# Weight and slab loads in paced pieces of 128 to 256 KB in place of transfers of 512 KB to 1 MB

## The chip, the cores and the metric

One core of one Trainium2 chip. The time is that of the device for one execution, in microseconds (us), the median of several runs; lower is better. One execution of each kernel was also profiled, and the trace of that execution is what the views below read.

## The reference

A transformer layer in bf16, batch 1, 2048 tokens of width 1024: attention with 32 query heads of 32 and one shared key and value head, then a gated feed-forward of width 3584.

```python
h  = x + A(layernorm(x))          # A: q = x@wq, k = x@wk, v = x@wv, softmax(q k^T / sqrt(32)) v, then @ wo
h2 = h + B(layernorm(h))          # B: (sigmoid(x@w_gate) * (x@w_up)) @ w_down
```

## The kernel before

The kernel holds a list scheduler in Python. It builds the instruction list of each engine ahead of time, from assumed durations, and then emits the five lists with semaphore waits. TensorE interleaves scores (`S_ps`), P·V blocks and the feed-forward, so that ScalarE's exponentials (`Pr<-S_ps`) never lack work. The feed-forward goes in 8 chunks of 256 tokens, and each chunk reads all of `w_gate` and `w_up` again: 14 slabs of 1 MB per chunk (a gate half and an up half of 512 KB), through a ring of five slabs. A slab is requested when the one five before it has been used:

```python
def load_wd(f, n, deps):                       # 7 times, 1 MB each
    wd_ld.append(dma(lambda: SP.dma_start(
        wd_sb[:, f:f + n, :], B_w_down[f * P:(f + n) * P, :].rearrange("(a p) n -> p a n", p=P)),
        f"wd{f}", n * P * D * 2, deps, prio=4))

def load_slab(s, deps):                        # 112 times, two transfers of 512 KB
    ...
    for w, W in ((0, B_w_gate), (1, B_w_up)):
        ops.append(dma(lambda w=w, W=W: SP.dma_start(
            wgu[:, sl, w, :, :], W[:, pi * SW:(pi + 1) * SW].rearrange("(a p) f -> p a f", p=P)),
            f"sl{sl}{w}", D * SW * 2, deps, prio=4))

def after(b, last):                            # after a gate (w == 0) or up (w == 1) group
    if w == 0:
        ...                                    # tanh on ScalarE
        return [tanh_of[s]]
    e = ...                                    # (tanh + 1) * up on VectorE
    load_slab(s + NSLAB, [last])               # both halves together
```

All these transfers are issued by SyncE, in the order of its list. Nothing in the kernel asks for instructions: the trace shows 189 fetches of 16 KB, spread over the run, in a DMA queue of their own (q8, 3.10 MB). They keep step with TensorE: in 200 to 250 us it starts 2,370 matmuls and weight loads and there are 9 fetches, in 1100 to 1150 us 785 and 3; over the run it is one fetch per 255 (48,282 by 189).

The softmax here doesn't subtract the row's maximum and nothing guards it: scores larger than these inputs give would overflow.

## Time and profile before

| | before |
|---|---|
| time, median of the first 3 runs (lowest to highest) | 1196.02 us (1194.79 to 1198.01) |
| profiled execution: span, granted TensorE clock | 1192.8 us, 0.997 |
| exponentials (1024), mean | 1035 ns |
| slab matmuls (3584), mean | 274 ns |
| slab loads, issue to landing, median | gate 4.1, up 5.5 us |

The prediction below shows the lines of the profile that matter. One habit helps in reading them: the share of busy time says which engine is the bound (TensorE, 95%), and the waits of that engine, the small ones too, say what there is to gain. Waits of other engines need not cost anything: here VectorE waits 213.6 us for TensorE's blocks (`Oc<-F_ps`) while TensorE is busy for 95%.

### The profile page before, as it was taken

What the parts mean: (1) busy time and instruction counts of PE and PEld (TensorE: products, weight loads), DVE (VectorE), ACT (ScalarE), POOL (GpSimd) and SP (SyncE); (2) the same over time, 40 slices, a digit from 0 to 9 for tenths busy, and PEclk for the clock granted to TensorE, in tenths of its full rate; (3) what the DMA queues carried; (4) which work ended last, traced back from release to release, by engine and by line L of the source; (5) the groups of instructions that cost most, each with busy time, mean ns of one, the idle gap of its engine ahead of it and who ended that gap; (6) DMA issues with size and microseconds to landing.
All of it is one profiled execution on the core that took longest, in us unless ns stands there. A gap on an engine that the chain in (4) does not pass through costs nothing.

```text
span 1192.8 us, 52074 instructions
## 1 busy us (share of the span) xinstructions
PE 1138.6 (95%) x24020; PEld 775.2 (65%) x24141; DVE 843.1 (71%) x1539; ACT 1041.8 (87%) x1188; POOL 50.4 (4%) x84
## 2 busy tenths in 40 slices
PE   8899899999999999999998899999999999999998
PEld 5745577776576756775576655776576746775784
DVE  8677767787887678777776678777868787776221
ACT  6799899999998999999998999999999999995110
POOL 4100000000000000000000000000000000000000
PEclk9999999999999999999999999999999999999999
DMA  8765501665155632655054652656155723654470
GB/s 247 188 198 154 170 21 47 181 173 130 43 160 140 179 82 71 178 165 147 25 151 136 162 117 58 186 146 172 29 152 149 186 58 98 182 159 111 126 210 18
DMA packets 286025, 158.15 MB, mean 133 GB/s; under 512 B 34672, under 2 KB 276336, under 8 KB 285808
## 3 DMA queue, kind: packets, MB, share of 16 engines
q1 hardware_dynamic: 283728, 154.69, 47.7%
q8 instruction: 189, 3.10, 1.1%
q10 hardware_dynamic: 2080, 0.13, 0.1%
q14 instruction: 28, 0.23, 0.1%
HBM read 140.64 MB, written 7.34 MB: 124 GB/s over the span
## 4 chain that ended last, share of the span: by engine, by line
PE 83%; ACT 6%; DVE 5%; issue 4%; DMA 1%; POOL 1%; SPq 0%; DVEq 0%
PE F_ps L348 70%; PE S_ps L348 13%; ACT Pr L547 5%; DVE Ts L565 1%; DMA hnT<-hn 1%; DVE st L289 1%; DVE st L291 1%; POOL dsb L308 0%; DMA ring<-in_A_x_dram 0%; DVE Oc L610 0%; DVE Oc L608 0%; DVE ring L328 0%; POOL zb L303 0%; ACT ring L332 0%; POOL rstd L310 0%
## 5 line engine op out<-in xcount | busy, mean ns | idle before, releaser
L547 ACT ACTIVATE Pr<-S_ps 128x1024 bf16<-128x1024 f32 x1024 | 969.2, 1035 | 45.4 <-PE S_ps L348 44.5
L348 PE MATMUL F_ps<-hnT,ring 128*128 128x256 bf16 x3584 | 441.8, 274 | 9.3 <-issue 4.4
L348 PEld LDWEIGHTS F_ps<-hnT,ring 128*128 128x128 bf16 x3584 | 330.7, 98 | 76.4 <-issue 12.3
L565 DVE TENSOR_TENSOR Ts<-Pr 128x1024 bf16<-128x1024 bf16 x512 | 342.1, 683 | 14.8 <-ACT Pr L547 10.7
L348 PE MATMUL S_ps<-QTb,kT 32*128 32x128 bf16 x8192 | 209.9, 217 | 20.8 <-issue 16.7
L348 PEld LDWEIGHTS S_ps<-QTb,kT 32*128 32x128 bf16 x8192 | 119.7, 93 | 149.1 <-ACT Pr L547 67.4
L348 PE MATMUL F_ps<-zone,hact 128*128 128x512 bf16 x822 | 199.5, 380 | 6.2 <-issue 5.3
L608 DVE COPY Oc<-F_ps 128x256 f32<-128x256 f32 x128 | 54.3, 424 | 213.7 <-PE F_ps L348 213.6
L565 DVE TENSOR_TENSOR Ts<-Ts 128x1024 bf16<-128x1024 bf16 x256 | 170.5, 667 | 1.5
L348 PE MATMUL F_ps<-Pr,Vb 128*32 128x128 bf16 x8192 | 138.7, 220 | 2.1 <-issue 1.3
L348 PEld LDWEIGHTS F_ps<-zone,hact 128*128 128x128 bf16 x896 | 78.9, 98 | 90.8 <-issue 1.2
L348 PEld LDWEIGHTS F_ps<-Pr,Vb 128*32 128x32 bf16 x8192 | 115.8, 97 | 25.1 <-issue 8.1
L737 ACT ACTIVATE tnh<-F_ps 128x512 f32<-128x512 f32 x112 | 67.6, 603 | 65.0 <-PE F_ps L348 64.8
L610 DVE RECIPROCAL Oc<-Oc 128x128 f32<-128x128 f32 x128 | 121.1, 946 | 0.2
L741 DVE SCALAR_TENSOR_TENSOR hact<-tnh,F_ps 128x512 bf16<-128x512 f32 x112 | 76.0, 678 | 54.7 <-PE F_ps L348 53.5
L348 PE MATMUL F_ps<-zone 128*128 128x256 bf16 (+2 forms) x497 | 71.1, 287 | 5.9 <-ACT QTb L235 2.2
L348 PE MATMUL F_ps<-wo_sb,OT 128*128 128x512 bf16 x227 | 58.7, 381 | 3.1 <-issue 2.5
L348 PEld LDWEIGHTS F_ps<-zone 128*128 128x128 bf16 x512 | 38.0, 97 | 28.4 <-ACT QTb L235 3.0
L303 POOL TENSOR_SCALAR zb<-mvb 128x1 bf16<-128x1 bf16 (+1 forms) x25 | 10.3, 414 | 1057.1 <-DVE mvb L299 1057.1
L348 PE MATMUL F_ps<-Ts,ones 128*32 128x128 bf16 x2048 | 51.5, 219 | 1.9 <-issue 1.9
L348 PE MATMUL F_ps<-kT,ident 128*128 128x256 bf16 x337 | 43.9, 279 | 0.0
L773 DVE SCALAR_TENSOR_TENSOR h_sb<-F_ps,h_sb 128x512 bf16<-128x512 f32 x32 | 21.6, 676 | 30.6 <-PE F_ps L348 30.2
(44 smaller groups left out, 341.3 us busy)
## 6 DMA issues: line engine op xcount, KB each, us to landing
ring<-in_B_w_gate_dram SPq DMA_DIRECT2D x112, 512.0 KB, 4.1
ring<-in_B_w_up_dram SPq DMA_DIRECT2D x112, 512.0 KB, 5.5
zone<-in_B_w_down_dram SPq DMA_DIRECT2D x7, 1024.0 KB, 7.0
h_sb<-in_A_x_dram SPq DMA_DIRECT2D x16, 256.0 KB, 2.7
out_dram<-h_sb SPq DMA_DIRECT2D x32, 128.0 KB, 1.7
q_scratch<-hact SPq DMA_DIRECT2D x24, 128.0 KB, 3.1
QTb<-q_scratch SPq DMA_DIRECT2D x6, 512.0 KB, 4.0
ring<-in_A_x_dram SPq DMA_DIRECT2D x5, 512.0 KB, 7.0
```

The lines of the kernel that those rows point to most:

```text
L289: a = pl.op("dve", lambda k=k, src=src: DVE.bn_stats(st[:, k, 0, :], src[:, 0:512]), dep, prio=prio, occ=590, lat=756, order=[st_user.get(k)])
L291: b = pl.op("dve", lambda k=k, src=src: DVE.bn_stats(st[:, k, 1, :], src[:, 512:1024]), dep, prio=prio, occ=590, lat=756, order=[st_user.g ...
L303: f = pl.op("pool", lambda: POOL.tensor_scalar(out=zb[:, ph, sl].unsqueeze(2), in0=mvb[:, ph, sl, 1:2], scalar1=LN_EPS_BF16, scalar2=None, ...
L348: return lambda: PE.matmul(o, lhsT=l, rhs=r, start=start, stop=stop, **kw)
L547: exps[u] = pl.op("act", lambda slot=slot, pb=pb: ACT.activation(out=Pr[:, slot, :].rearrange("p (a b) -> p a b", a=2), in_=S_ps[:, pb:pb ...
L565: return pl.op("dve", lambda: DVE.tensor_tensor(out=out, in0=a, in1=b, op=ALU.add), deps, prio=prio, **t_dve(1024, 1.92))
L608: cp = pl.op("dve", lambda: DVE.tensor_copy(out=Oc[:, k, :], in_=F_ps[:, b, 0:2 * P]), [last, o_ev.get(G - 2)], prio=0, **t_dve(256))
L610: a = pl.op("dve", lambda: DVE.reciprocal(Oc[:, k, P:2 * P], Oc[:, k, P:2 * P]), [cp], prio=2, occ=880, lat=1020)
L737: tanh_of[s] = pl.op("act", lambda: ACT.activation(out=tnh[:, k, 0:2 * n], in_=F_ps[:, b, 0:2 * n], func=ACTF.Tanh, scale=0.5), [last, tn_ ...
L741: e = pl.op("dve", lambda: DVE.scalar_tensor_tensor(out=hactT[:, 2 * pi:2 * pi + 2, 0:n], in0=tnh[:, k, 0:2 * n].rearrange("p (a b) -> p a ...
L773: e = pl.op("dve", lambda: DVE.scalar_tensor_tensor(out=h_sb[:, t % 4, sl], in0=F_ps[:, b, :], scalar=0.5, in1=h_sb[:, t % 4, sl], op0=ALU ...
```

## The change

The intent: send the same bytes in small pieces, one at a time and evenly, so that no long burst fills the DMA engines. A piece is put into a queue; the scheduler takes one out every `nbytes / 145` ns and makes it wait for the latest exponential done by then. Besides, each half of a slab is now requested as soon as that half has been used.

```diff
+    DPP = 2
+    PACE = 145.0
+        def pace(fn, key, nbytes, deps, sink):
+            paced.append((fn, key, nbytes, deps, sink))
+
+        def pump(t):
+            while paced and t >= next_piece[0]:
+                fn, key, nbytes, deps, sink = paced.popleft()
+                ...                            # clock[0]: the latest exponential that has ended by t
+                beat = exps[clock[0]] if clock[0] in exps and clock[0] + 1 in exps else pl.lists["pe"][-1]
+                sink.append(dma(fn, key, nbytes, list(deps) + [beat], prio=4))
+                next_piece[0] = max(next_piece[0] + nbytes / (PACE if v < NV - 8 else 300.0), t - 1000.0)
...
         def load_wd(f, n, deps):
-            wd_ld.append(dma(...))                                # 1 MB
+            for i in range(f, f + n):
+                pace(lambda i=i: SP.dma_start(wd_sb[:, i, :], B_w_down[i * P:(i + 1) * P, :]), f"wd{f}", P * D * 2, deps, wd_ld)
...
-        def load_slab(s, deps):
+        def load_slab(s, w, deps):
...
+            for d in range(0, DT, DPP):
+                pace(lambda d=d: SP.dma_start(
+                    wgu[:, sl, w, d:d + DPP, :],
+                    W[d * P:(d + DPP) * P, pi * SW:(pi + 1) * SW].rearrange("(a p) f -> p a f", p=P)),
+                    f"sl{sl}{w}", P * DPP * SW * 2, deps, slab_ld[(s, w)])
...
             def after(b, last):
+                load_slab(s + NSLAB, w, [last])
...
-                load_slab(s + NSLAB, [last])
...
+            pump(t)                                               # once per step of the scheduler
```

The output weights are cut up like `load_wd`, and the gates of the groups wait until all pieces of a load have been issued.

More of the change, by code (lines that the diff above doesn't have):

```diff
@@ L224, in dma @@
             return pl.op(ring, fn, deps, occ=occ, key=key, nbytes=nbytes, prio=prio)
+        paced = collections.deque()
+        next_piece = [0.0]
+        exps = {}
+        clock = [0]
+        def pace(fn, key, nbytes, deps, sink):
[3 more added lines that the diff above has]
+                fn, key, nbytes, deps, sink = paced.popleft()
+                while clock[0] + 1 in exps and exps[clock[0] + 1].end is not None and exps[clock[0] + 1].end <= t:
+                    clock[0] += 1
+                beat = exps[clock[0]] if clock[0] in exps and clock[0] + 1 in exps else pl.lists["pe"][-1]
+                sink.append(dma(fn, key, nbytes, list(deps) + [beat], prio=4))
+                next_piece[0] = max(next_piece[0] + nbytes / (PACE if v < NV - 8 else 300.0), t - 1000.0)
         def evac(fn_act, fn_dve, n, deps, prio, dve_rate=0.96):
@@ L455, in load_wd @@
         def load_wd(f, n, deps):
-            wd_ld.append(dma(lambda: SP.dma_start(
-                wd_sb[:, f:f + n, :], B_w_down[f * P:(f + n) * P, :].rearrange("(a p) n -> p a n", p=P)),
-                f"wd{f}", n * P * D * 2, deps, prio=4))
+            for i in range(f, f + n):
+                pace(lambda i=i: SP.dma_start(wd_sb[:, i, :], B_w_down[i * P:(i + 1) * P, :]), f"wd{f}", P * D * 2, deps, wd_ld)
         wo_ld = []
@@ L464, in early_loads @@
             if n in (10, 12):
-                k = len(wo_ld)
-                wo_ld.append(dma(lambda: SP.dma_start(
-                    wo_sb[:, 4 * k:4 * k + 4, :], A_wo[k * 512:(k + 1) * 512, :].rearrange("(g p) n -> p g n", p=P)),
-                    f"wo{k}", D * D, [last, xT_ev[NT - 1]], prio=4))
+                k = (n - 10) // 2
+                for g in range(4 * k, 4 * k + 4):
+                    pace(lambda g=g: SP.dma_start(wo_sb[:, g, :], A_wo[g * P:(g + 1) * P, :]), f"wo{k}", P * D * 2,
+                         [last, xT_ev[NT - 1]], wo_ld)
             if n in (14, 18, 22, 26, 30):
-                load_slab((n - 14) // 4, [last] + list(xT_pe.values()))
+                for w in range(2):
+                    load_slab((n - 14) // 4, w, [last] + list(xT_pe.values()))
         wd_left = list(range(7))
@@ L500, in bass_sequential_preLN__grouped_kv_mqa__glu_gated_glu__prompt_kernel @@
         NV = len(visits)
-        exps = {}
         slot_of = {}
@@ L680, in mk_OP @@
             gr = Group("OP", atoms, lambda: [o_ev[t * NG + g] for g in range(NG)] + [xr_ld[t]] + wo_ld, after)
-            gr.gate = lambda: len(wo_ld) == 2 and t in xr_ld and (t < 2 or (t - 2) in hT_ev)
+            gr.gate = lambda: len(wo_ld) == NG and t in xr_ld and (t < 2 or (t - 2) in hT_ev)
             return gr
@@ L700, in flush_hT @@
                             queues["GU"].append(mk_GU(c, pi, w))
-        slab_ld = {}
-        def load_slab(s, deps):
+        slab_ld = collections.defaultdict(list)
+        def load_slab(s, w, deps):
             if s >= len(CH) * NFT // 2:
@@ L708, in load_slab @@
             sl = s % NSLAB
-            ops = []
-            for w, W in ((0, B_w_gate), (1, B_w_up)):
-                ops.append(dma(lambda w=w, W=W: SP.dma_start(
-                    wgu[:, sl, w, :, :], W[:, pi * SW:(pi + 1) * SW].rearrange("(a p) f -> p a f", p=P)),
-                    f"sl{sl}{w}", D * SW * 2, deps, prio=4))
-            slab_ld[s] = ops
+            W = (B_w_gate, B_w_up)[w]
+            for d in range(0, DT, DPP):
[3 more added lines that the diff above has]
+                    f"sl{sl}{w}", P * DPP * SW * 2, deps, slab_ld[(s, w)])
         hact_ev = {}
@@ L730, in atoms @@
                         r.append((mm(F_ps[:, b, f * n:(f + 1) * n], wgu[:, sl, w, dt, f * P:(f + 1) * P], hnT[:, dt, 0:n],
-                                     dt == 0, dt == DT - 1), n, [slab_ld[s][w]] if f == dt == 0 else []))
+                                     dt == 0, dt == DT - 1), n, slab_ld[(s, w)] if f == dt == 0 else []))
                 return r
@@ L754, in after @@
                 return [e]
-            gr = Group("GU", atoms, lambda: [hT_ev[t] for t in CH[c]] + [slab_ld[s][w]], after)
-            gr.gate = lambda: s in slab_ld and (q_left[0] == 0 if c == 0 else d_done[c - 1] == 2 * len(CH[c - 1]))
+            gr = Group("GU", atoms, lambda: [hT_ev[t] for t in CH[c]] + slab_ld[(s, w)], after)
+            gr.gate = lambda: len(slab_ld[(s, w)]) == DT // DPP and (q_left[0] == 0 if c == 0 else d_done[c - 1] == 2 * len(CH[c - 1]))
             return gr
@@ L780, in after @@
                 return [e]
-            return Group("D", atoms, lambda: list(wd_ld) + [ev[ft] for ft in range(NFT - 6)], after)
+            gr = Group("D", atoms, lambda: list(wd_ld) + [ev[ft] for ft in range(NFT - 6)], after)
+            gr.gate = lambda: len(wd_ld) == NFT
+            return gr
         for t in range(NT):
```

## The prediction

> **What bounds the kernel now.** I read the page first: busy time, then the chain that ended last, then the DMA queues.
>
> ```profile
> PE 1138.6 (95%) x24020; PEld 775.2 (65%) x24141; DVE 843.1 (71%) x1539; ACT 1041.8 (87%) x1188; POOL 50.4 (4%) x84
> ...
> q1 hardware_dynamic: 283728, 154.69, 47.7%
> q8 instruction: 189, 3.10, 1.1%
> ...
> PE 83%; ACT 6%; DVE 5%; issue 4%; DMA 1%; POOL 1%; SPq 0%; DVEq 0%
> ```
>
> TensorE is the bound. DMA moves data only half of the time and is 1% of the chain, so no load is late. Two entries look minor and are the ones I follow: 4% of the chain is "issue" (TensorE waits for nothing that the profile shows), and there is a queue of 189 instruction fetches. 3.10 MB / 189 is 16 KB a fetch. TensorE runs 24,020 matmuls and 24,141 weight loads; [...]
>
> Next the list of waits for TensorE (matmuls, then weight loads), whole run:
>
> ```profile
> PE S_ps L348 <- issue: 16.7, 33, 2.5
> PE F_ps L348 <- issue: 16.4, 61, 2.0
> PEld S_ps L348 <- issue: 69.1, 257, 2.6
> PEld F_ps L348 <- issue: 24.2, 52, 2.2
> ```
>
> Columns: total us, times, longest. Most of these waits are a 0.2 us bubble at a switch between kinds of matmul, but a few last 2 us. (Weight-load and matmul rows overlap; they must not be added.) I then looked at the long ones, of which two are shown: that at 682.7 in TensorE's timeline (start, us, what, idle before it); that at 367.9 in the busy time of three stretches around it (length; PE, PEld, DVE, ACT, POOL busy; granted clock; DMA share; GB/s); and for the first again the DMA queues of 682.0 to 682.5 (packets, MB, share):
>
> ```profile
> 682.29 0.40 PE L348 MATMUL S_ps<-QTb,kT 32*128 32x128 bf16 x16
> 684.69 1.48 PE L348 MATMUL F_ps<-hnT,ring 128*128 128x256 bf16 x12 [1.99 <-issue]
> ```
> ```profile
> 365.30:367.30 2.00, 2.00 (x101) 1.57 (x100) 0.93 (x2) 2.00 (x3) 0.00 (x0) 1.00 1.04 267
> 367.40:369.40 2.00, 0.52 (x16) 0.23 (x15) 1.29 (x2) 0.65 (x1) 0.00 (x0) 1.00 0.00 0
> 369.40:371.40 2.00, 1.54 (x9) 1.05 (x9) 0.89 (x3) 1.22 (x2) 0.00 (x0) 0.60 0.04 8
> ```
> ```profile
> q1 hardware_dynamic: 115, 0.05, 44.2%
> q8 instruction: 1, 0.02, 14.1%
> ```
>
> In both cases the pattern is one and the same. A gate and an up slab (512 KB each, issued 0.4 us apart) fill the DMA engines for about 4 us; just as that burst drains, one instruction fetch starts (682.2 and 367.4); about 2.5 us later TensorE goes on. Laying all fetches of the trace beside the bytes moved in the 2 us before each (160 to 1095 us): of 45 fetches with under 60 KB before them 2 are followed by a stall over 0.4 us, of 88 with over 400 KB 24 are. Nineteen of the 20 stalls over 0.6 us have the burst's end within some 0.5 us of the fetch's start. So I read: the fetch queues behind whatever slab bytes were issued before it, and TensorE runs dry, most of all after a P·V block, which eats about 128 instructions in 1.1 us.
>
> The same stalls do a second damage. The clock sits at half speed for 3.4 us right after the two long ones at 144.0 (2.51 us) and 367.9 (1.94 us):
>
> ```profile
> 147.90:151.30 3.40, 3.40 (x32) 2.07 (x30) 0.96 (x2) 2.76 (x3) 0.00 (x0) 0.50 0.01 2
> 369.80:373.20 3.40, 3.35 (x27) 2.14 (x30) 2.54 (x5) 1.94 (x2) 0.00 (x0) 0.50 0.40 114
> ```
>
> [...] an exponential takes 1034 ns at 160 to 200 us (23 GB/s) and 1031 ns at 205 to 250 us (about 180 GB/s), and a slab matmul 273 and 274 ns. So spreading the loads won't speed up any instruction. [...]
>
> **The change, part by part.**
>
> *Order.* I compared the two built programs: TensorE, ScalarE, VectorE and GpSimd run the same instructions in the same order, down to the 337 filler matmuls on kT. Only SyncE's list differs. Whatever is gained must be waits of TensorE, not work.
>
> *Transfers.* 224 slab loads of 512 KB become 896 of 128 KB; 7 down-projection loads of 1 MB become 28, and 2 output-weight loads of 1 MB become 8, of 256 KB. Rows stay 512 B and 2 KB, so packets stay as they are. The Q loads (6 of 512 KB) are untouched in the diff, in spite of the description. SyncE issues about 700 more transfers; a store of the same 128 KB takes 0.34 us to issue (332/338/357 ns), so some 240 us more of an engine that has over 700 us to spare. That costs nothing by itself.
>
> *Removed from the path.* The chain in order of time has 23 "issue" pieces of 0.45 us or more between 139 and 1069 us, 20.8 us in all. Three of them (372.9, 457.0, 457.6; 1.36 us) do not follow a fetch. The other 20 make 19.4 us; less the ordinary 0.2 us bubble that stays, 19.4 − 4.0 = **15.4 us**.
>
> *Clock.* Two spells of 3.4 us at half clock cost at most 1.7 us each: **up to 3.4 us**.
>
> *Transposes.* The hnT transposes land 3.0/3.1/4.9 us (least, median, most) after issue; the one of 4.87 us at 459 is on the chain. With a short queue ahead it should take 3.1: **1.8 us**.
>
> *Added.* In the middle a piece is issued per 0.9 us (128 KB at 145 GB/s, the rate in the diff), about one per exponential of 1.035 us. At the roughly 300 GB/s that bursts show, a piece occupies the engines 0.44 us. A fetch may still wait that long. In the tail, after the last exponentials, pieces go at 300 GB/s; the last chunk needs nine 1 MB slabs in about 44 us (213 GB/s), and the half-slabs are now requested as soon as each half is used, so I put nothing there.
>
> *Sum.* 15.4 + 3.4 + 1.8 = 20.6 us at best. I take off a quarter: for fetches that still meet a piece, and because ScalarE, 1041.8 us busy and nearly without a gap in 200 to 250 us (50.00 of 50), takes over part of the path once TensorE stops stalling. Remaining gain 15.5 us: 1196.0 − 15.5 ≈ **1180 us** (−1.3%).
>
> **The rivals.**
> (a) *Rate, not backlog, delays the fetch.* Then an even 145 GB/s (290 KB per 2 us) puts every fetch in the middle class of my table: of 29 fetches with 60 to 400 KB ahead of them 4 stalled, 1.8 us in all, 0.06 us each; times some 160 fetches that is 10 us against today's 21. Gain about 8 to 10 us with the clock: 1187 us. Against it: the fetches start when the burst ends.
> (b) *Loads come late, or block the in-order SyncE queue.* Each piece waits for an exponential; a transpose or store behind it waits too, and a slab may land after TensorE wants it. Even 145 GB/s is above the mean need (117 MB of slabs over about 1000 us), but in the slab stages slices of the page show up to 190. The ring holds five slabs, 5 MB, and 79 us at 190 GB/s overdraw it by about 3.6 MB, so it should hold; the last 80 us are the tightest. If it doesn't hold: new waits on ring loads at 8 chunk ends of 1 to 2 us, 1190 to 1205 us.
> (c) *ScalarE is already the bound.* Removing TensorE's stalls would then only lengthen its waits for exponentials (67.4 us today in 173 waits of up to 0.4): gain under 6 us, 1190 us. For it: 87% busy overall, 95% and more in many stretches. Against it: the stretches with the stalls (600 to 640: TensorE 37.26, ScalarE 37.08 of 40) have both idle together.
>
> **Range and chances.** The full sum without discount and a few small bubbles more gives 1172; rivals (a) and (c) give 1187 to 1190. So 1172 to 1191. Faster by 2% means below 1172, nearly the whole sum: 0.11. Slower by 2% needs (b) in earnest: 0.02. The rest is within 2%: 0.87.
>
> **What would show it.** Right: "issue" on the chain falls from about 43 us to about 25; no TensorE wait on issue of over 1 us after 100 us; granted clock 1.00 at 148 and 370; fetches still 189; exponentials still 1035 ns; transposes all near 3.1 us. Wrong: issue pieces as many as before though shorter (a), waits on ring or hnT in the list (b), or waits on exponentials grown by what issue lost (c).

## The result, and the profile after

| | before | after |
|---|---|---|
| time, median (lowest to highest; runs) | 1195.4 us (1194.39 to 1198.01; 4) | 1164.49 us (1164.2 to 1164.64; 4) |
| profiled execution: span, granted clock | 1192.8 us, 0.997 | 1162.5 us, 1.000 |
| TensorE busy | 1138.6 us (95%) | 1149.5 us (99%) |
| exponentials, mean | 1035 ns | 1037 ns |
| slab matmuls, mean | 274 ns | 273 ns |

The ratio is 0.9738, 95% interval 0.9721 to 0.9755. Ratios here are the mean time of one kernel's fast runs over that of the other's fast runs of the same rounds, so not quite the ratio of the medians. All runs are in the fast state or count as such. The kernel is 31 us faster, where 15.5 us were predicted.

The page of the changed kernel, the lines that answer to the first ones of the prediction:

```profile
PE 1149.5 (99%) x24141; PEld 772.2 (66%) x24141; DVE 841.0 (72%) x1539; ACT 1038.3 (89%) x1188; POOL 50.1 (4%) x84
...
q1 hardware_dynamic: 294912, 154.73, 49.0%
q8 instruction: 189, 3.10, 1.1%
...
PE 91%; DVE 4%; ACT 3%; POOL 1%; DMA 1%; issue 1%; DVEq 0%; POOLq 0%
```

The same bytes and the same 189 fetches, but "issue" has fallen from 4% to 1% of the chain. The waits of TensorE's weight loads in the changed kernel (total us, times, longest):

```profile
PEld S_ps L368 <- issue: 55.2, 245, 0.4
PEld F_ps L368 <- issue: 11.6, 38, 0.8
```

The longest were 2.6 and 2.2 us before. The many short ones stay; those in 200 to 300 us of the changed kernel take 0.21 to 0.23 us each, at the switch from one kind of matmul to another. The place that stalled for 1.99 us at 682.7, and the two places where the clock fell to half, in the changed kernel (they come earlier there; timeline of TensorE, then stretches with the columns of the prediction):

```profile
659.91 0.40 PE L368 MATMUL S_ps<-QTb,kT 32*128 32x128 bf16 x16
660.25 1.59 PE L368 MATMUL F_ps<-hnT,ring 128*128 128x256 bf16 x13
```
```profile
143.20:146.60 3.40, 3.40 (x58) 2.68 (x57) 3.37 (x7) 3.40 (x5) 0.00 (x0) 1.00 0.49 157
356.10:359.50 3.40, 3.40 (x51) 2.79 (x44) 2.53 (x5) 3.40 (x6) 0.00 (x0) 1.00 0.70 194
```

The slab matmuls follow the scores without a gap: they start 0.34 us after them, where it was 2.40 us before (682.29 to 684.69), so this place alone gives 2.06 us. And the granted clock is 1.00 with the loads running beside (157 and 194 GB/s).

**Where the 30 us went, exactly.** Both programs have the same 24,141 weight loads in the same order, and both traces recorded all of them. So the start of each weight load in one trace can be subtracted from its start in the other. The difference rises only in steps, and their sum is the difference of the spans:

| part | us |
|---|---|
| 2 stalls at 140.0 and 146.5 us (0.94 and 2.73) | 3.7 |
| 30 stalls from 351 us on (0.07 to 2.20 each) | 23.7 |
| the two half-clock spells (the rest of the steps at 146.5 and 369.9: 1.52 and 1.47) | 3.0 |
| one transpose at the start of a chunk (4.87 us before, 4.40 after) | 0.5 |
| first 35 us (the changed kernel is a little later) | −0.6 |
| sum | 30.3 |

Each of the 32 stalls ends 2.2 to 2.8 us after the start of an instruction fetch. Between the steps the two kernels keep pace to within 0.3 us: nothing that was won is given back. The fetch is late, not slow: the transfer of one takes 1.13 us (median) before and 1.06 after.

One warning on reading: the trace of before has 24,020 matmul records and that of after 24,141, of 24,141 executed. The 121 missing ones show as short "issue" pieces, so the total of "issue" on the chain (43 us before, 7 after) overstates the gain. The weight loads are complete in every trace of this study, so I compare those.

### The profile page after: what moved, and what is told of

It is laid out like the page before. It is cut to its first block, busy times and chain, and to the rows that moved or that the text cites. A ratio compares the mean times of both kernels' runs of the same rounds, so it can differ in the third digit from the quotient of the medians.

```text
span 1162.5 us, 53018 instructions
## 1 busy us (share of the span) xinstructions
PE 1149.5 (99%) x24141; PEld 772.2 (66%) x24141; DVE 841.0 (72%) x1539; ACT 1038.3 (89%) x1188; POOL 50.1 (4%) x84
## 4 chain that ended last, share of the span: by engine, by line
PE 91%; DVE 4%; ACT 3%; POOL 1%; DMA 1%; issue 1%; DVEq 0%; POOLq 0%
PE F_ps L368 76%; PE S_ps L368 15%; ACT Pr L566 2%; DVE Ts L584 1%; DMA hnT<-hn 1%; POOL dsb L328 1%; DVE Oc L629 0%; DMA zone<-ring 0%; DVE Oc L627 0%; POOL zb L323 0%; POOL rstd L330 0%; DVE hn L337 0%; DVE st L309 0%; DVE st L311 0%; DVE h_sb L689 0%
## 5 line engine op out<-in xcount | busy, mean ns | idle before, releaser
L566 ACT ACTIVATE Pr<-S_ps 128x1024 bf16<-128x1024 f32 x1024 | 966.1, 1037 | 18.1 <-PE S_ps L368 17.4
L368 PE MATMUL F_ps<-zone,hact 128*128 128x512 bf16 x896 | 218.1, 380 | 0.0
L368 PEld LDWEIGHTS S_ps<-QTb,kT 32*128 32x128 bf16 x8192 | 118.1, 92 | 134.0 <-ACT Pr L566 67.0
L368 PE MATMUL S_ps<-QTb,kT 32*128 32x128 bf16 x8192 | 205.9, 217 | 0.1
L368 PE MATMUL F_ps<-zone 128*128 128x256 bf16 (+2 forms) x512 | 74.6, 289 | 4.0 <-ACT QTb L255 2.2
L368 PE MATMUL F_ps<-wo_sb,OT 128*128 128x512 bf16 x256 | 65.3, 381 | 0.0
```

The source lines that it names most:

```text
L368: return lambda: PE.matmul(o, lhsT=l, rhs=r, start=start, stop=stop, **kw)
L566: exps[u] = pl.op("act", lambda slot=slot, pb=pb: ACT.activation(out=Pr[:, slot, :].rearrange("p (a b) -> p a b", a=2), in_=S_ps[:, pb:pb ...
```

## The experiments

In all of them the instruction order on TensorE, ScalarE, VectorE and GpSimd was compared with that of the kernel before and is the same; only SyncE's list differs. (e5 also drops semaphore waits: TensorE has 82 of them, the others 293.) So each trace can be laid over that of the changed kernel as above. The results in one table: time and ratio against the kernel before (same chip, same rounds), and how far each kernel's profiled execution is behind the changed kernel in three parts of it (100 to 155 us holds the early loads; after it come the slab stages).

| kernel | us, median | ratio (95%) | 0–100 | 100–155 | after 155 |
|---|---|---|---|---|---|
| before | 1195.4 | 1 | −0.6 | 5.2 | 25.6 |
| the change | 1164.5 | 0.974 (0.972–0.976) | 0 | 0 | 0 |
| e1 pieces, unpaced, half release | 1169.7 | 0.981 (0.978–0.983) | −0.3 | 3.9 | 2.4 |
| e2 paced, whole transfers | 1170.1 | 0.981 (0.978–0.984) | 1.2 | 1.2 | 3.3 |
| e3 half release alone | 1173.3 | 0.984 (0.981–0.987) | −0.1 | 4.8 | 7.1 |
| e5 no slab reload (wrong result) | 1169.6 | 0.981 (0.979–0.983) | −0.4 | 3.3 | 2.4 |
| e8 pieces, unpaced, joint | 1170.3 | 0.980 (0.979–0.982) | 0.1 | 3.7 | 1.9 |
| e4 early loads paced alone | 1187.6 | 0.996 (0.994–0.997) | −0.4 | 0.0 | 23.2 |
| e6 paced at 290 GB/s | 1168.1 | 0.979 (0.978–0.981) | 0.3 | 1.5 | 1.8 |
| e9 paced, joint | 1165.0 | 0.976 (0.975–0.978) | −0.6 | 0.0 | 0.3 |
| e11 double bursts | 1200.4 | 1.007 (1.004–1.009) | −0.1 | 4.6 | 24.2 |
| e12 pieces of 256 KB, unpaced, joint | 1173.2 | 0.985 (0.982–0.987) | −0.5 | 3.9 | 4.3 |
| e7 paced pieces of 256 KB | 1165.8 | 0.978 (0.976–0.981) | 0.3 | 0.1 | 0.9 |

"Joint" means that both halves of a slab are requested together, as before; "half release" that each is requested after its own use. The kernel before was at 1192.9, 1192.8 and 1191.9 us on the three chips of the experiments, so compare ratios across them. Kernels with stalls scatter by some us from run to run (e1: 1166.38 to 1170.84), the changed kernel by 0.4.

My theory, the **backlog theory**: a fetch is served after the bytes that were issued before it and have not been moved yet; TensorE has about 2 us of instructions in hand (an estimate of mine: it lies between the median delays measured below, 2.6 us for the fetches that end in a stall and 0.6 for the others), and what exceeds that is a stall. The rivals: a **saturation theory** (the fetch waits as long as the engines are full), a **pacing theory** (only the low even rate helps) and that the stalls have nothing to do with the slab traffic.

The expectations below use these figures: bursts moved 302 and 314 GB/s in the kernel before (680.5 to 682 and 364.5 to 367 us), so by estimate, at 300 GB/s, 128 KB take 0.44 us, 256 KB 0.87, 512 KB 1.75 and 1 MB 3.5; the issue of a 128 KB store took SyncE 0.34 us and that of a gate half 0.37 (medians). The slack of about 2 us is the estimate above.

### Is it the slab traffic? (e5)

```diff
 def load_slab(s, deps):
+    if s >= NSLAB:
+        slab_ld[s] = slab_ld[s - NSLAB]
+        return
```

> Wrong result on purpose: the kernel before without any slab reload (the first five slabs are used for all), so hardly any DMA traffic after 160 us. Early loads unchanged. If slab traffic costs only through instruction fetches: the early stalls (about 5.2 us with the clock) stay, the other 25 us go, about 1170 us, and no issue wait of over 0.6 us after 160 us that follows a fetch. If traffic costs something else too (slower instructions, late transposes): below 1167 us. If the stalls have nothing to do with the slab traffic: near 1195 us.

Measured 1169.56 us, as expected. No fetch-linked stall is left after 155 us: the early 3.3 us stay. The 2.4 us in the last column are something else, one transpose that took 4.88 us with no slab load near it, and the half-clock spell after it. That the total came out as expected is in part chance: the early stalls cost 3.3 us and not 5.2, as no half-clock spell follows them here, and the transpose fills the gap. The stretch after that wait, first, and then the times of all transposes of the hnT tile, in e5 and in the changed kernel:

```profile
586.00:589.40 3.40, 3.40 (x30) 2.14 (x29) 0.51 (x1) 1.94 (x2) 0.00 (x0) 0.50 0.27 77
```
```profile
DMA to landing us min/median/max: 3.0/3.1/4.9
```
```profile
DMA to landing us min/median/max: 3.0/3.1/4.4
```

So a slow transpose does not need the slab queue: one came without it (4.9 us), and one of 4.4 us with paced pieces.

### Do the stages add? (e4)

The early loads (down-projection, output weights, first five slabs) in paced pieces, all reloads as before:

```diff
-                load_slab(s + NSLAB, w, [last])            # paced pieces
...
+                reload_slab(s + NSLAB, [last])             # two transfers of 512 KB, after the second half
```

> The change for the early loads alone (down-projection, output weights and the first five slabs in paced pieces); all slab reloads as 512 KB pairs as in the kernel before. If the gains of the stages add: only the two stalls at 140 and 146 us and the half-clock spell at 148 us go, 5.2 us, 1187 to 1190 us, and the stalls after 160 us stay as they were.

Measured 1187.58 us, in the range (1187 to 1190); the trace shows 0.0 us left at 100 to 155 and 23.2 us after it. The stages add.

### Which part of the change does it? (e1, e2, e3, e9)

e1 takes the pacing away and keeps the pieces:

```diff
 def pace(fn, key, nbytes, deps, sink):
-    paced.append((fn, key, nbytes, deps, sink))
+    sink.append(dma(fn, key, nbytes, deps, prio=4))
```

> The pieces of 128 and 256 KB, but each issued as soon as its buffer is free: no even rate, no tie to the exponentials. Compute order on all engines is unchanged. Backlog theory (a fetch waits for the bytes issued before it and not yet moved): SyncE needs 0.34 to 0.37 us to issue a piece and the DMA engines 0.44 us to move it, so over the four or eight pieces of a burst the backlog grows to some 0.5 us only; most stalls vanish, 1166 to 1174 us. Saturation theory (a fetch waits as long as the engines are full): the burst of a freed half-slab is still about 1.8 us of full engines, stalls shrink but remain, 1178 to 1190 us. Pacing theory (the even rate is what helps): near the kernel before, 1190 us or more.

e2 takes the pieces away and keeps the pacing and the earlier request (`DPP = 8`, and 1 MB for the two other weights, each through `pace`):

> The pacing alone: whole transfers of 512 KB (slab halves) and 1 MB (down-projection and output weights), one at a time at 145 GB/s, tied to the exponentials. Backlog theory: at most 1.75 us of bytes lie ahead of a fetch in the slab stages in place of 3.5 us, so of the 32 stalls of the kernel before only those over 1.75 us leave a rest; the 1 MB transfers around 144 us keep part of theirs: 1167 to 1174 us. If the piece size is what matters (one long transfer holds the fetch up to its end): 1178 to 1190 us.

e3 is the kernel before with the earlier request alone:

```diff
 def after(b, last):
+    load_slab(s + NSLAB, w, [last])            # its own half, 512 KB
     if w == 0:
...
-    load_slab(s + NSLAB, [last])
```

> The kernel before with one line of the change: each slab half is requested as soon as its own half has been used, not both together after the second. Transfers stay 512 KB and 1 MB, unpaced. Backlog theory: in the slab stages a burst is 512 KB and 1.75 us long, so most of the stalls after 160 us go, the early ones (5.2 us with the half-clock spell at 148 us) stay, and the stalls of reloads that lie close together stay: 1170 to 1178 us. If piece size or pacing is needed: 1190 us or more.

e9 is the changed kernel with the request put back to where it was:

```diff
-                load_slab(s + NSLAB, w, [last])
...
+                for h in range(2):
+                    load_slab(s + NSLAB, h, [last])        # both, after the second half
```

> The changed kernel without the earlier request: both halves of a slab are handed to the pacing together after the second use. Backlog theory: the pacing keeps the queue short whatever the time of the request, 1163 to 1167 us. If the earlier request is needed on top (slabs late, or larger clumps of pieces): 1168 us or more, with waits on slab loads in the last 80 us or new issue waits.

Measured: e1 1169.74, e2 1170.06, e3 1173.33, e9 1165.01 us, all within what the backlog theory said; the pacing theory falls with e1 and e3. No single part is needed for most of the gain in the slab stages (25.6 us lost before): the earlier request alone leaves 7.1 us, with the pacing of whole transfers added 3.3, with unpaced pieces added 2.4; unpaced pieces alone leave 1.9 (e8 below). The pacing of whole transfers without the earlier request was not run, so what pacing does alone there is not shown. (The profiled run of e3 was the slowest of its four, 1176.24 us; the others took 1170.66 to 1174.39.) Pacing with pieces leaves nothing (0 and 0.3), whenever the halves are requested. What the pacing still does alone is seen in the early loads: e1 keeps 3.9 us of 5.2 there. It issues the four 256 KB pieces of a down-projection load back to back; eleven of them went out in 6.2 us from 134.0 on (465 GB/s, above the 300 of the bursts), which is a backlog again.

### Backlog or saturation? (e8, e11, e12)

e8: the pieces, unpaced and joint. The same 1 MB is released at the same point as before:

> Pieces of 128 KB, unpaced, and both halves of a slab requested together after its second use, as in the kernel before: a burst of eight pieces, 1 MB, as long as before. SyncE's list of the unpaced pieces shows 2.0 us for four (0.5 us each, 262 GB/s), a little less than the engines can move, so the engines are about as full and as long as in the kernel before, but hardly anything lies queued. Backlog theory: as the unpaced pieces with half release, 1166 to 1174 us. Saturation theory (a fetch waits while the engines are full, whatever is queued): most of the 25 us of stalls in the slab stages stay, 1183 us or more.

Measured 1170.32 us, and 1.9 us left after 155 us. SyncE hands the pieces over no faster than they are moved. How long an issue took it (ns, least/median/most), before and in e8:

```profile
L711 SPq DMA_DIRECT2D ring<-in_B_w_gate_dram x112: 367/368/1473, 55.3 to 1148.3; - x112
L711 SPq DMA_DIRECT2D ring<-in_B_w_up_dram x112: 372/584/2833, 55.7 to 1149.6; - x112
```
```profile
L730 SPq DMA_DIRECT2D ring<-in_B_w_gate_dram x448: 367/469/2004, 56.2 to 1132.4; - x150
L730 SPq DMA_DIRECT2D ring<-in_B_w_up_dram x448: 368/470/2042, 58.1 to 1134.4; - x150
```

Before, 1 MB was handed over in about 1 us and took some 3.5 us to move (an estimate from the 300 GB/s of the bursts). In pieces, 128 KB per 0.47 us is 279 GB/s, no more than the bursts show. There is a limit to this test: the bursts of e8 are also a little less full than those of before, so it does not rule out saturation alone. e11 does more of that. It doubles the burst (both halves of two slabs after every second use, 2 MB):

```diff
-                load_slab(s + NSLAB, [last])
+                if s % 2 == 1:
+                    load_slab(s + NSLAB - 1, [last])
+                    load_slab(s + NSLAB, [last])
```

> More of the suspected cause: the kernel before with the slabs requested two at a time after every second use, 2 MB in one burst of four transfers, half as many bursts, the same bytes. Compute order is unchanged on all engines. Backlog theory: twice the bytes may lie ahead of a fetch, and what exceeds the slack of about 2 us grows much more than twofold: stalls up to 4 us and more, 1205 to 1260 us. If stalls go with the total time of full engines, or come from something other than the loads: within 1% of the kernel before, 1185 to 1205 us.

Measured 1200.37 us, 0.7% slower than before: outside the range of the backlog theory (1205 to 1260) and inside the rival's (1185 to 1205). The profiled run (1192.93 us, the fastest of the seven) has 24.2 us of loss after 155 us, against 25.6 before. So in this run the loss did not grow with the bytes released at once, and the longest step was 2.5 us, not 4; the four runs at 1200 to 1201 us took some 8 us more, and no trace of them was kept. Per burst the loss did double (24.2 us over 54 bursts, 25.6 over 107). SyncE's list of e11 shows what my expectation forgot, the third and fourth transfer of a burst being held up at issue:

```profile
748.53 0.37 SPq L711 DMA_DIRECT2D ring<-in_B_w_gate_dram  x1
748.94 0.58 SPq L711 DMA_DIRECT2D ring<-in_B_w_up_dram  x1
749.56 1.08 SPq L711 DMA_DIRECT2D ring<-in_B_w_gate_dram  x1
750.69 1.58 SPq L711 DMA_DIRECT2D ring<-in_B_w_up_dram  x1
```

I read this so: the bytes ahead of a fetch do not go from 1 to 2 MB. This reading was made after the result. But the saturation theory is hit harder, by the same burst. Busy time of three stretches of 1 us of e11, the DMA queues of the first of them, and TensorE's timeline:

```profile
755.00:756.00 1.00, 0.80 (x14) 0.39 (x13) 1.00 (x4) 0.99 (x2) 0.00 (x0) 1.00 1.22 298
756.00:757.00 1.00, 0.00 (x0) 0.00 (x0) 1.00 (x3) 0.00 (x0) 0.00 (x0) 1.00 1.00 254
757.00:758.00 1.00, 0.09 (x7) 0.09 (x6) 0.23 (x1) 0.00 (x0) 0.00 (x0) 1.00 0.10 27
```
```profile
q8 instruction: 1, 0.02, 7.6%
```
```profile
755.46 0.34 PE L348 MATMUL S_ps<-QTb,kT 32*128 32x128 bf16 x9
757.91 0.29 PE L348 MATMUL S_ps<-QTb,kT 32*128 32x128 bf16 x7 [2.11 <-issue]
```

The fetch starts at 755.34 with the engines full before and after it (298 and 254 GB/s), and TensorE resumes 2.57 us later. So this fetch got its turn in the middle of a full stream; it did not wait for the stream to end. Over the whole trace: before, 74 of the 107 bursts after 200 us have a fetch starting 4.5 to 5.5 us after the first issue, just where the 1 MB has drained, and only 14 have one at 1 to 4.5 us. In e11 most starts spread from 4.5 to 9 us.

The traces also bound the moment at which a fetch is asked for. TensorE's list is the same in all kernels but e5, so I take it that the n-th fetch is asked for at the same place of that list in each of them; this is an assumption. Then it is asked for at the latest where the earliest of these twelve kernels starts it. Call that the asking point. In the kernel before, between 160 and 1095 us, 66 fetches had over 400 KB handed over and not yet moved at their asking point. They start 2.2 us (median) after it, and 47 of them within 0.5 us of the moment at which these bytes have been moved. 62 fetches had under 60 KB before them and start 0.26 us (median) after it. The fetches that end in a stall start 2.6 us after their asking point in the median, the others 0.6; the estimate of about 2 us in hand lies between. The fetch at 755.34 above was asked for by 751.79, with 0.99 MB handed over and unmoved; these had been moved at 755.11. That fits a place in a line. It is no exact line, though: in e11 and e12 such fetches start 1.4 and 1.2 us (median) before all that had been handed over has been moved.

e12 raises the piece of e8 to 256 KB, so that SyncE is faster than the engines again (at 600 us of its trace, two pieces are handed over in 0.92 to 1.06 us, 495 to 570 GB/s):

```diff
-    DPP = 2
+    DPP = 4
```

> As the unpaced joint pieces, but of 256 KB: SyncE issues a piece in about 0.5 us while the engines need 0.87 us to move it, so within a burst of four the queue builds up again, to some 1.5 us. Backlog theory: between the unpaced 128 KB pieces (1170 us) and the kernel before: 1173 to 1185 us. If only the length of a single transfer counts (a fetch waits for the one in progress, at most 0.9 us): as the 128 KB pieces, 1167 to 1172 us.

Measured 1173.22 us: at the lower edge of the range, and 4.3 us left after 155 us, against 1.9 in e8 and 25.6 before. The direction is as expected; the fetches with over 400 KB before them are 1.4 us late here in the median, where it was 2.2, which lies mostly within the estimated 2 us that TensorE has in hand.

### How sharp is the choice of 128 KB and 145 GB/s? (e6, e7)

`PACE = 290.0` (e6):

> The changed kernel with the even rate doubled from 145 to 290 GB/s: pieces about 0.45 us apart, tied to the exponentials as before. Backlog theory: a piece is drained in 0.44 us, so at most one or two pieces lie ahead of a fetch: 1164 to 1168 us, as the change. If the low rate itself is what keeps fetches fast: 1172 us or more.

`DPP = 4`, paced as in the change (e7):

> The changed kernel with slab pieces of 256 KB, four to a slab, still one at a time at 145 GB/s. Backlog theory: at most 0.87 us lie ahead of a fetch, under its slack of about 2 us: 1164 to 1167 us, as with 128 KB. If pieces have to be 128 KB: 1169 us or more.

Measured 1168.05 us, just at the upper end of its range (1164 to 1168), and 1165.84 us, inside its own. Not sharp: twice the piece costs about 1 us, twice the rate about 3.5 (of which 1.5 in the early loads, whose 256 KB pieces then come about as fast as they drain: 0.90 us apart at 290 GB/s, 0.87 to move by the estimate above). No version was found that beats the changed kernel; e9 is level with it.

The waits of weight loads on "issue" tell the same story in one line each. In 160 to 1060 us, in this order: before, e4, e11; then e8, e9, the changed kernel:

```profile
PEld F_ps L348 <- issue: 23.4, 49, 2.2
```
```profile
PEld F_ps L368 <- issue: 25.2, 51, 2.1
```
```profile
PEld F_ps L348 <- issue: 21.6, 45, 2.4
```
```profile
PEld F_ps L368 <- issue: 11.8, 38, 0.8
```
```profile
PEld F_ps L368 <- issue: 11.5, 37, 0.8
```
```profile
PEld F_ps L368 <- issue: 11.2, 37, 0.8
```

The floor of about 11 us in 37 waits (0.3 us each in the mean, 0.8 at most) is there without any fetch stall as well; what lies above it, in waits of up to 2.4 us, I put down to the fetches.

## Why the prediction was right or wrong

**The mechanism was right.** In the kernel before, 32 stalls of TensorE (27.4 us) follow the start of an instruction fetch by 2.2 to 2.8 us; without the slab reloads (e5) none is left after 155 us, and the change removes these 27.4 us and nothing else of weight. Fetches stay 189, instructions do not get faster or slower (slab matmuls 274 and 273 ns, exponentials 1035 and 1037), no wait on a slab load appears, the clock is 1.00 at both places, and the long waits on issue are gone.

**The size was wrong by a factor of two** (30.9 us gained, 15.5 forecast). The step that failed is the term *Removed from the path*, and with it the discount on the sum. Term by term:

- *Removed from the path: 15.4 us said, 27.4 us measured.* Three errors, all downward. The 20 listed pieces of the chain made 19.4 us, but the same 20 places moved by 23.5 us when the traces are laid over each other. A piece of the chain starts at the modelled end of the last matmul and so leaves out about 0.2 us of each stall. I took 0.2 us off each where 0.2 us should have been added; that alone is 8 us. And I listed only pieces of 0.45 us or more: 12 smaller stalls of 0.07 to 0.56 us make another 3.8 us. They were there to be found, since all of them follow a fetch by 2.4 to 2.8 us.
- *Clock: up to 3.4 us said, 3.0 measured.* Right.
- *Transposes: 1.8 us said, 0.5 measured.* The step "with a short queue ahead it should take 3.1" failed: transposes of 4.4 us occur with paced pieces and of 4.9 without any slab reload. What slows single ones is open.
- *The discount of a quarter, 5.1 us: none of it was due.* Fetches that still meet a piece cost little (e7, with pieces twice as long, loses about 1 us), and ScalarE did not take over: its waits for scores fell from 44.5 to 17.4 us while TensorE's weight loads waited as long for exponentials as before (67.4 and 67.0 us). That is rival (c) disproved. The two engines had stood still together, and moved up together.

**Rival (a)**, that the rate delays a fetch, is disproved by e6 (290 GB/s, 1168.05 us) and e8 (unpaced, 1170.32 us), where it put 1187 us at 145 GB/s; **rival (b)**, late loads, by the absence of any wait on a slab load and by e9, which requests later still and loses nothing. The forecast of rival (a) has a slip of its own: 10 us of 21 leave a gain of 11 before the clock, not 8 to 10 with it. Nor did the packets "stay as they are": 283,728 became 294,912. The 235,520 of 512 B and the 8,704 of 2 KB did stay; the added ones are of 4 bytes, 16 for each of the 699 added transfers, without a visible cost.

**Range and chances.** The lower end of the range, 1172, lay 3.4 us below the undiscounted sum (1196.0 − 20.6 = 1175.4), so a gain of 2% needed more than the whole sum, not "nearly" all of it. That sum was itself too small, so the range had no room on the side where the result fell, and the chance of "faster" (0.11) was too low. A check that would have caught it stands in the prediction itself: rival (a) counts 21 us of such stalls today, and only 15.4 were entered.

**Open.** Why the other runs of e11 (four of seven at 1200 to 1201 us) are 7 to 8 us slower than its profiled one; three of them show a lower granted clock (0.993 to 0.994 against 0.997), the fourth does not. Why a stall of about 2.5 us is followed by a half-clock spell in some kernels (before, where one of 2.51 us at 144.0 is followed by 3.4 us at half clock; e1, e3, e11, e12) and not in others (e5 and e8 at the same place). How the place of a fetch in the line is decided: no trace shows the moment at which it is asked for, only the bound above; nor is it known why fetches in e11 and e12 start before all that was handed over has been moved.

## What to carry to other kernels

Here the instruction stream is a DMA customer too: 189 fetches of 16 KB, of which 32 end in a stall of TensorE, 27.4 us of 1195. Where a core runs as many instructions as this one (48,000 on TensorE), look in the trace at what the longest "issue" waits of the bounding engine have in common: if they end a fixed time after an instruction fetch, as here (2.2 to 2.8 us), try to shorten what stands ahead of it. Here it was enough for most of the gain to release a load in halves or in pieces, and for all of it to pace pieces of 128 KB (256 KB cost about 1 us more, e7); the bytes did not shrink. With the DMA engines busy for half of the time (q1 47.7% before, 49.0% after), 896 slab pieces of 128 KB in place of 224 of 512 KB brought no wait on a slab load. And size such a gain by laying two traces of the same instruction order over each other, or, beforehand, by whole gaps between starts, not by idle pieces from which the usual gap is taken off.
